# Attention on one core: normalisation steps a period later, one weight step a period, all row sums from a pre-added tile

## The chip, the core and the metric

The kernel runs on one core of a Trainium2 chip. The time is in device microseconds of that core. A profiled execution gives one trace; times in the trace count from the start of its span.

## What is computed

The program chains three stages in float32: an attention with a soft cap, a dense feed-forward layer and a layer with eight experts, of which each token uses one. The change touches the attention alone.

```python
# q, k, v: (4, 12, 448, 64), cap = 30
scores = scale * np.matmul(q, k.transpose(0, 1, 3, 2))
scores = cap * np.tanh(scores / cap)
scores = scores - np.max(scores, axis=-1, keepdims=True)
attn = np.exp(scores)
attn = attn / (np.sum(attn, axis=-1, keepdims=True) + 1e-09)
return np.matmul(attn, v).astype(np.float32)
...
h = x @ w_in                          # x: 1792 tokens x 768
g = np.maximum(h, 0.0) ** 2
x = g @ w_out
```

The kernel leaves out the maximum: with the cap, exp(30) is the most that can come, and the small term 1e-9 is scaled by exp(-cap) to fit (`eps`).

## The kernel before

**Pairs and periods.** The 48 heads are worked on as 24 pairs, `pr` = 0 to 23; two heads of 64 rows fill 128 partitions. A loop with `pr` = 0 to 24 makes the scores of pair `pr` and, one turn late, the values of pair `pr - 1`. A turn of this loop is called a period here. Its instructions are recorded engine by engine in the order of the code, and each engine and each queue works in that order; semaphores make an engine wait for what it needs.

**One period on each engine.** The keys of a head are cut in four chunks: three of 128 keys (one pair of heads gives two score tiles each, `scores`, L198) and a last one of 64, where both heads share one tile (`scores_last`, L213). q and k come as float32 and are split into a high and a low part (`prep`, L61 and L63, on VectorE), so each score is three matmuls. ScalarE takes tanh of the scores from PSUM (L204, L218), and one exp over all seven tiles of a pair (`exps`, L224). TensorE multiplies by the values (`values_last`, L241; `values`, L248) and, with a stationary tile of ones, makes the row sums of exp (L257) in the other half of the same PSUM tile. ScalarE copies one head's result out (`copy_out`, L266, tile `ot`), VectorE the other's (L269, into `x`). Only two PSUM tiles `o` exist, so the next pair's L241 waits for both copies.

**The fold.** VectorE adds chunks of exp together before TensorE sums them (`fold`, L232, tile `w`): where two chunks are added, one add is done and TensorE has two pairs of `ones` matmuls (`o<-t,ones` for the third chunk, `o<-w,ones`); where three are added, two adds and one pair. Before the change three are added in the odd periods below 16, two in the others.

**Normalisation in units of four heads.** `norm_sum` gathers each head's sums through SP in a small tile `den` (L287) and moves the odd head's result to its place in `x` (L289). Then `norm_recip` adds `eps` and takes the reciprocal (L349, L350, VectorE), `norm_spill` writes it to DRAM (`dd`, L354, SP), `norm_spread` reads it back broadcast over 64 partitions (`r`, L362, SP, two DMAs), and `norm_x` multiplies `x` by it (L369, VectorE, two instructions for a unit). The table `when` gives, in half periods, how long after its heads each step is recorded. A step for an even number stands after `values` and ahead of `prep` in the code of its period; one for an odd number stands at the period's end.

**Other work in the attention.** The table `side` puts steps of the feed-forward layer's first weights into periods: three chunks, each with two loads and six steps on VectorE (`w_steps`: L400 to L410 and the split), and six splits of `x` for the first group of tokens (`split_x`). SP also issues the loads of the next pairs: `qkraw` (L177) and `v` (L183).

```python
last = NHD // NU - 2
for u in range(last + 1):
    i0 = NU * (u + 1) + 2
    when = (1, 1, 2, 5, 6)
```

Of the kernel before, what the change touches and what calls it, by code (L numbers as in the profile page):

```python
# [10 lines left out]
F32 = mybir.dt.float32  # L11
# [4 lines left out]
ALU = mybir.AluOpType  # L16
# [4 lines left out]
B, H, S, D = 4, 12, 448, 64  # L21
NHD = B * H
# [7 lines left out]
KC = 4  # L30
KP = 128
KL = S - (KC - 1) * KP
NP, NPC = NHD // 2, 2 * (KC - 1) + 1
QK = S + KC * KP
FOLD_ALL = 32
FB = 2
NU = 4
WARM = 8
# [10 lines left out]
class Kernel:  # L49
# [13 lines left out]
        eng.tensor_tensor(out=lo, in0=src, in1=f32(hi), op=ALU.subtract)  # L63


    def constants(self):
        nc, tc = self.nc, self.tc
        p = self.const
        cap = p.tile([128, 1], F32, name="cap")
        nc.sync.dma_start(out=cap, in_=self.a["cap"].rearrange("(o n) -> o n", o=1).to_broadcast([128, 1]))  # L70
        self.cap = cap

    def scales(self):
        nc, p, cap = self.nc, self.const, self.cap
        self.tscale = p.tile([128, 1], F32, name="tscale")
        nc.vector.reciprocal(out=self.tscale, in_=cap)
        nc.vector.tensor_scalar_mul(out=self.tscale, in0=self.tscale, scalar1=float(D) ** -0.5)
        self.eps = p.tile([128, 1], F32, name="eps")
        nc.scalar.activation(out=self.eps, in_=cap, func=ACTF.Exp, scale=-1.0)
        nc.vector.tensor_scalar_mul(out=self.eps, in0=self.eps, scalar1=1e-9)  # L80

    def gate_loads(self):
        nc = self.nc
# [59 lines left out]
    def attention(self, tail_p):  # L143

        nc, tc, a = self.nc, self.tc, self.a
        with ExitStack() as ctx:
            pool = lambda name, bufs, **k: ctx.enter_context(tc.tile_pool(name=name, bufs=bufs, **k))
            raw_p = pool("araw", 2)
            hl_p = pool("ahl", 2)
            t_p = pool("at", 2)  # L150
            w_p = pool("aw", 2)
# [20 lines left out]
            def load(pr, cuts=(0, QK)):  # L172
                if pr < NP:
                    b, j = divmod(pr, H // 2)
                    raws[pr] = raw_p.tile([128, QK], F32, tag="qk", name="qkraw")
                    for c0, c1 in zip(cuts, cuts[1:]):
                        nc.sync.dma_start(out=raws[pr][:, c0:c1], in_=a["qk"][b, j, :, c0:c1])  # L177

            def load_v(pr):
# [5 lines left out]
            def prep(pr, cuts=(0, QK)):  # L185

                if pr < NP:
                    t = raws.pop(pr)
                    w = hls[pr] = hl_p.tile([128, 2, QK], F32R, tag="hl", name="hl")
                    for c0, c1 in zip(cuts, cuts[1:]):  # L190
                        self.split("dve", "dve", w[:, 0, c0:c1], w[:, 1, c0:c1], t[:, c0:c1])

            def scores(pr, c):

# [28 lines left out]
                t = P[pr]  # L223
                nc.scalar.activation(out=t, in_=t, func=ACTF.Exp, scale=self.cap[:KP])  # L224

            def fold(pr, chunks):

                if chunks > 1:
                    W[pr] = w_p.tile([KP, 2, S], F32, tag="w", name="w")
                    src = P[pr][:, 0:2]  # L230
                    for c in range(1, chunks):
                        nc.vector.tensor_tensor(out=W[pr], in0=src, in1=P[pr][:, 2 * c:2 * c + 2], op=ALU.add)  # L232
                        src = W[pr]


            def values_last(pr):
# [3 lines left out]
                for h, o in enumerate(sums[pr]):  # L240
                    nc.tensor.matmul(out=o, lhsT=last[rows[h]], rhs=P[pr][rows[h], NPC - 1], start=True, stop=False)  # L241

            def values(pr, chunks):

                v, p, o = vs.pop(pr), P.pop(pr), sums[pr]
                for c in range(KC - 1):
                    for h in range(2):
                        nc.tensor.matmul(  # L248
                            out=o[h][rows[h]], lhsT=v[:, 2 * c + h], rhs=p[:, 2 * c + h],
                            start=False, stop=c == KC - 2,  # L250
                        )
                parts = [p[:, 2 * c:2 * c + 2] for c in range(chunks, KC - 1)]
                if chunks > 1:
                    parts.append(W.pop(pr))
                for n, t in enumerate(parts):
                    for h in range(2):
                        nc.tensor.matmul(  # L257
                            out=o[h][rows[1 - h]], lhsT=one, rhs=t[:, h], start=False, stop=n == len(parts) - 1
                        )

            def copy_out(pr, h):
                i = 2 * pr + h
# [7 lines left out]

            cuts = (0, S + KP, QK)
            load(0, cuts)
            self.constants()
            load_v(0)
            load(1)
            load_v(1)
            prep(0, cuts)
            self.scales()
            load(2)
            den = []  # L280

# [11 lines left out]
            last = NHD // NU - 2  # L293
            for u in range(last + 1):
                i0 = NU * (u + 1) + 2
                when = (1, 1, 2, 5, 6)
                for j, f in zip(when, (
                    lambda u=u: self.norm_recip(den[u]),
                    lambda u=u: dd.update({u: self.norm_spill(den[u])}),
                    lambda u=u: r.update({u: self.norm_spread(n_p if u < last else tail_p, dd[u])}),  # L300
                    lambda u=u: self.norm_x(u, r[u], (0,)),
                    lambda u=u: self.norm_x(u, r[u], (1,)),
                )):
                    if u < last or j < 3:
                        steps.setdefault(i0 + j, []).append(f)

            prep(1)
            for pr in range(NP + 1):  # L310
                i = 2 * pr
                chunks = 3 if pr % 2 == 1 and i < FOLD_ALL else 2
                if pr:
                    fold(pr - 1, chunks)
                for c in range(KC - 1):
                    if pr and c == KC - 2:
                        values_last(pr - 1)
                    if pr < NP:
                        scores(pr, c)
                    if not pr and not c:  # L320
                        scores_last(pr)
                if pr < NP:
                    exps(pr)
                if pr:
                    values(pr - 1, chunks)
                    copy_out(pr - 1, 1)
                scores_last(pr + 1)
                for f in steps.get(i, []) + self.side.get(i, []):
                    f()
                prep(pr + 2)  # L330
                if pr:
                    copy_out(pr - 1, 0)
                    if pr % 2:
                        p, bufs = (tail_p, 1) if pr == NP - 1 else (n_p, 2)
                        den.append(p.tile([128, NU * S // 128], F32, tag="den", name="den", bufs=bufs))
                else:
                    load(3)
                load(pr + 4)
                if pr:
                    norm_sum(i - 2)  # L340
                    norm_sum(i - 1)
                load_v(pr + 2)
                for f in steps.get(i + 1, []) + self.side.get(i + 1, []):
                    f()
# [463 lines left out]
def build(ctx, tc, a, stop=None):  # L808
# [9 lines left out]
    with tc.manual_schedule():  # L818
# [10 lines left out]
        k.dram = pool("adr", 2, space=DRAM)  # L829
        tail_p = tc.alloc_tile_pool(name="tail", bufs=1, side="right")  # L830
        side = k.side = {6: [k.gate_loads]}
        at = iter([i for i in range(NU, NHD) if i % NU in (0, 1)])
        chunks = [k.w_steps(*c) for c in (("i", 0), ("i", 1), ("o", 0))]
        side[2] = [chunks[0][0]]
        for n, (_, *rest) in enumerate(chunks):
            for m, f in enumerate(rest):
                i = next(at)
                side.setdefault(i, []).append(f)
                if m == len(rest) // 2 and n + 1 < len(chunks):
                    side[i].append(chunks[n + 1][0])  # L840
        for j, i in enumerate((34, 35, 38, 39, 42, 43)):
            side.setdefault(i, []).append(lambda j=j: k.split_x(0, "dve", "dve", j))
        conv = k.w_conv(*k.chunk(0))
        side.setdefault(43, []).append(lambda: k.w_load(*k.chunk(0)))
# [41 lines left out]
def _layout(i):  # L886
    c = np.ascontiguousarray
    pair = lambda t: t.transpose(0, 1, 3, 2).reshape(B, H // 2, 2 * D, t.shape[2])
    q, k, v = i["q"], i["k"], i["v"]
    n = (KC - 1) * KP  # L890
    last = pair(k[:, :, n:])
    z = np.zeros_like(last[:, :, :D])
    last = np.concatenate([np.concatenate([last[:, :, :D], z], 3), np.concatenate([z, last[:, :, D:]], 3)], 2)
    qk = np.concatenate([pair(q), pair(k[:, :, :n]), last], 3)
    vl = v[:, :, n:].reshape(B, H // 2, 2, KL, 1, D)
    one = np.ones_like(vl[:, :, 0])
    vl = np.concatenate([np.concatenate([vl[:, :, 0], one], 3), np.concatenate([one, vl[:, :, 1]], 3)], 2)
    v = v[:, :, :n].reshape(B, H // 2, 2, KC - 1, KP, D).transpose(0, 1, 4, 3, 2, 5).reshape(B, H // 2, KP, -1, D)
    w_in = c(c(i["moe_w_in"]).reshape(KD, 128, NFC, 128).transpose(2, 1, 0, 3))
    return {  # L900
        "qk": c(qk),
        "v": c(np.concatenate([v, vl], 3)),
        "cap": c(i["cap"]).reshape(1),
        "w_in": w_in.view(np.int64),
        "w_out": c(i["moe_w_out"]).view(np.int64),
        "mod_id": c(c(i["moe2_modality_id"]).reshape(NT // 128, 128).T),
        "w_gate": c(c(i["moe2_w_gate"]).reshape(KD, 128, E).transpose(1, 0, 2)),
        "mod_bias": c(i["moe2_modality_bias"]),
        "w1": c(i["moe2_w1"].reshape(E, KD, 128, NF2, 128).transpose(0, 3, 2, 1, 4)).reshape(E, NF2, 128, DM),
        "w2": c(  # L910
            i["moe2_w2"].reshape(E, NF2 // 2, 2, 128, 2, HALF).transpose(0, 4, 1, 3, 2, 5)
        ).reshape(E, 2, NF2 // 2, 128, DM),
    }
# [14 lines left out]
```

## Time and profile before

| | us |
|---|---|
| median of 3 runs (lowest, highest) | 910.21 (908.96, 910.98) |
| the profiled execution | 908.5 |
| its span | 906.8 |
| TensorE matmul busy | 889.1 (98%) |
| VectorE busy | 565.1 (62%) |
| ScalarE busy | 371.7 (41%) |

The span is the time from the first to the last instruction; the profiled execution is 1.7 us longer and lies within the runs. The shares are means over stages with different limits: in the attention, roughly the first 192 us, ScalarE and VectorE are far busier than over the whole. Matmul ends are modelled, so the starts of instructions are the better thing to read. In the timelines instructions of one kind that follow each other are one row, with their count behind the x; a float32 matmul of the attention's values or sums counts as two.

### The profile page before, as it was taken

Reading aid. Unit: us, or ns where it says so; the run is one execution under the profiler, and the core shown is the slowest. Engines: PE = TensorE matmul, PEld = TensorE weight load, DVE = VectorE, ACT = ScalarE, POOL = GpSimd, SP = SyncE. Lnnn points to the kernel's source line nnn. Section 1 sums busy time; section 2 is a strip of 40 time slices with the busy share of each in tenths; the row PEclk is TensorE's granted clock in tenths of the full one; section 3 lists DMA queues with packets and bytes.
Section 4 is the critical chain, followed back from the end, with each engine's and each line's share of the span. In section 5 each row is a group of like instructions: output and inputs, shape, how many; then the busy total and the mean of one; then the engine's idle time right before and its main releaser. Section 6 shows DMA issues by size and latency. Waiting matters only on the chain.

```text
span 906.8 us, 12105 instructions
## 1 busy us (share of the span) xinstructions
PE 889.1 (98%) x4674; PEld 734.5 (81%) x4675; DVE 565.1 (62%) x1067; ACT 371.7 (41%) x532; POOL 0.6 (0%) x9
## 2 busy tenths in 40 slices
PE   8999989999999999999999999999999999999997
PEld 4554444558989989889898898988978998999997
DVE  6768577667856767676676676554857516336361
ACT  7998878967542332413223232324421111111111
POOL 0000000000000000000000000000000000000000
PEclk9999999999999999999999999999999999999999
DMA  6554655432321111212121121000115424525451
GB/s 200 138 163 125 175 151 144 120 99 92 105 70 48 58 53 53 62 45 69 35 71 53 53 58 48 18 1 0 53 38 168 153 66 135 166 79 162 136 164 48
DMA packets 39571, 83.29 MB, mean 92 GB/s; under 512 B 8656, under 2 KB 16976, under 8 KB 39504
## 3 DMA queue, kind: packets, MB, share of 16 engines
q1 hardware_dynamic: 35472, 76.92, 28.8%
q10 hardware_dynamic: 4032, 5.51, 1.6%
q8 instruction: 39, 0.64, 0.3%
q14 instruction: 28, 0.23, 0.1%
HBM read 73.97 MB, written 5.59 MB: 88 GB/s over the span
## 4 chain that ended last, share of the span: by engine, by line
PE 90%; DVE 4%; ACT 2%; DMA 2%; issue 1%; SPq 0%; DVEq 0%; ACTq 0%
PE h L426 12%; PE h L428 12%; PE h L427 12%; PE y L426 8%; PE y L428 8%; PE y L427 8%; PE o L248 5%; PE o L426 4%; PE o L428 4%; PE o L427 4%; PE s L198 4%; PE o L257 3%; PE o L241 2%; PE s L213 2%; DMA den<-ot 2%
## 5 line engine op out<-in xcount | busy, mean ns | idle before, releaser
L428 PE MATMUL h<-xh,wil 128*128 128x512 f32 (+1 forms) x576 | 208.9, 363 | 0.0
L426 PE MATMUL h<-xh,wih 128*128 128x512 f32 (+1 forms) x576 | 208.8, 363 | 0.0
L427 PE MATMUL h<-xl,wih 128*128 128x512 f32 (+1 forms) x576 | 208.8, 362 | 0.0
L517 DVE TENSOR_TENSOR x<-y,x 128x512 f32<-128x512 f32 (+1 forms) x168 | 103.9, 622 | 70.0 <-PE y L428 68.9
L426 PE MATMUL y<-gh,woh 128*128 128x512 f32 (+1 forms) x384 | 139.6, 364 | 0.5 <-DVE x L517 0.4
L428 PE MATMUL y<-gh,wol 128*128 128x512 f32 (+1 forms) x384 | 139.2, 362 | 0.0
L427 PE MATMUL y<-gl,woh 128*128 128x512 f32 (+1 forms) x384 | 139.1, 362 | 0.0
L493 ACT ACTIVATE r<-h 128x512 f32<-128x512 f32 (+1 forms) x64 | 34.9, 545 | 243.3 <-PE h L428 236.8
L426 PEld LDWEIGHTS h<-xh,wih 128*128 128x128 f32 x576 | 108.2, 188 | 12.5 <-issue 0.7
L427 PEld LDWEIGHTS h<-xl,wih 128*128 128x128 f32 x576 | 108.1, 188 | 11.6
L428 PEld LDWEIGHTS h<-xh,wil 128*128 128x128 f32 x576 | 108.1, 188 | 11.3
L499 DVE TENSOR_TENSOR gl<-r,gh 128x512 fp32r<-128x512 f32 (+1 forms) x64 | 39.7, 621 | 64.8 <-ACT gh L498 64.8
L426 PEld LDWEIGHTS y<-gh,woh 128*128 128x128 f32 x384 | 72.1, 188 | 9.4 <-DVE x L517 0.9
L427 PEld LDWEIGHTS y<-gl,woh 128*128 128x128 f32 x384 | 72.1, 188 | 7.6
L428 PEld LDWEIGHTS y<-gh,wol 128*128 128x128 f32 x384 | 72.1, 188 | 7.5
L426 PE MATMUL o<-w2h,hh 128*128 128x384 f32 x224 | 74.9, 335 | 0.0
L428 PE MATMUL o<-w2h,hl 128*128 128x384 f32 x224 | 74.9, 334 | 0.0
L427 PE MATMUL o<-w2l,hh 128*128 128x384 f32 x224 | 74.9, 334 | 0.0
L204 ACT ACTIVATE t<-s,tscale 128x896 f32<-128x896 f32 x72 | 69.7, 1008 | 9.1 <-PE s L198 8.1
L224 ACT ACTIVATE t<-t,cap 128x3136 f32<-128x3136 f32 x24 | 69.8, 2910 | 0.8
L198 PE MATMUL s<-hl 64*128 64x448 f32 x432 | 62.8, 413 | 0.0
L727 DVE SCALAR_TENSOR_TENSOR hl<-h,hh 128x512 fp32r<-128x512 f32 (+1 forms) x32 | 19.9, 622 | 68.6 <-ACT hh L726 68.6
(122 smaller groups left out, 1022.6 us busy)
## 6 DMA issues: line engine op xcount, KB each, us to landing
raw<-w SPq DMA_DIRECT2D x64, 384.0 KB, 3.2
raw<-w_in SPq DMA_DIRECT2D x32, 384.0 KB, 3.1
raw<-w_out SPq DMA_DIRECT2D x32, 384.0 KB, 3.1
qkraw<-qk SPq DMA_DIRECT2D x23, 480.0 KB, 4.3
v<-v SPq DMA_DIRECT2D x24, 256.0 KB, 2.9
r<-dd SPq DMA_DIRECT2D x24, 224.0 KB, 3.8
out<-o ACTq DMA_DIRECT2D x28, 192.0 KB, 1.8
x<-ot SPq DMA_DIRECT2D x24, 112.0 KB, 2.2
```

The source lines that it names most:

```text
L198: nc.tensor.matmul(out=s[:, h, :S], lhsT=w[rows[h], kp, S + c * KP:S + (c + 1) * KP], rhs=w[rows[h], qp, :S], start=n == 0, stop=n == 2,)
L204: nc.scalar.activation(out=P[pr][:, 2 * c:2 * c + 2], in_=s[:, :, :S], func=ACTF.Tanh, scale=self.tscale[:KP])
L224: nc.scalar.activation(out=t, in_=t, func=ACTF.Exp, scale=self.cap[:KP])
L248: nc.tensor.matmul(out=o[h][rows[h]], lhsT=v[:, 2 * c + h], rhs=p[:, 2 * c + h], start=False, stop=c == KC - 2,)
L257: nc.tensor.matmul(out=o[h][rows[1 - h]], lhsT=one, rhs=t[:, h], start=False, stop=n == len(parts) - 1)
L426: nc.tensor.matmul(out=out, lhsT=wh, rhs=vh, start=first and j == 0, stop=False)
L427: nc.tensor.matmul(out=out, lhsT=wh, rhs=vl, start=False, stop=False)
L428: nc.tensor.matmul(out=out, lhsT=wl, rhs=vh, start=False, stop=last and j == m - 1)
L493: nc.scalar.activation(out=r, in_=ps, func=ACTF.Relu)
L499: split = lambda: nc.vector.tensor_tensor(out=gl, in0=r, in1=f32(gh), op=ALU.subtract)
L517: nc.vector.tensor_tensor(out=y, in0=ps, in1=y, op=ALU.add)
L727: nc.vector.scalar_tensor_tensor(out=hl, in0=ps, scalar=0.0, in1=f32(hh), op0=ALU.max, op1=ALU.subtract)
```

## The change

The three chunks are added in every period, so the branch on `chunks` falls away. The normalisation's steps come one half period later in the table (1, 1, 2, 5, 6 becomes 2, 2, 3, 8, 8, and 2, 2, 3, 7, 7 for the last units), which moves the reciprocal and the spill from the end of a period into the next one. The weight steps go from two in every second period to one in each, the splits of `x` two to four half periods later. The cap no longer has a DMA of its own: it comes as 16 columns ahead of q and k in the first pair's load, and the scales are made between the two cuts of that pair's split.

```diff
-FOLD_ALL = 32
+CP = 16
...
-                    raws[pr] = raw_p.tile([128, QK], F32, tag="qk", name="qkraw")
+                    raws[pr] = raw_p.tile([128, CP + QK], F32, tag="qk", name="qkraw")
                     for c0, c1 in zip(cuts, cuts[1:]):
+                        c0, c1 = CP + c0 if c0 or pr else 0, CP + c1
                         nc.sync.dma_start(out=raws[pr][:, c0:c1], in_=a["qk"][b, j, :, c0:c1])
...
-                        self.split("dve", "dve", w[:, 0, c0:c1], w[:, 1, c0:c1], t[:, c0:c1])
+                        self.split("dve", "dve", w[:, 0, c0:c1], w[:, 1, c0:c1], t[:, CP + c0:CP + c1])
+                        if not pr and not c0:
+                            self.scales(t[:, 0:1])
...
-            def fold(pr, chunks):
-
-                if chunks > 1:
-                    W[pr] = w_p.tile([KP, 2, S], F32, tag="w", name="w")
-                    src = P[pr][:, 0:2]
-                    for c in range(1, chunks):
-                        nc.vector.tensor_tensor(out=W[pr], in0=src, in1=P[pr][:, 2 * c:2 * c + 2], op=ALU.add)
-                        src = W[pr]
+            def fold(pr):
+
+                w = W[pr] = w_p.tile([KP, 2, S], F32, tag="w", name="w")
+                nc.vector.tensor_tensor(out=w, in0=P[pr][:, 0:2], in1=P[pr][:, 2:4], op=ALU.add)
+                nc.vector.tensor_tensor(out=w, in0=w, in1=P[pr][:, 4:6], op=ALU.add)
...
-                parts = [p[:, 2 * c:2 * c + 2] for c in range(chunks, KC - 1)]
-                if chunks > 1:
-                    parts.append(W.pop(pr))
-                for n, t in enumerate(parts):
-                    for h in range(2):
-                        nc.tensor.matmul(
-                            out=o[h][rows[1 - h]], lhsT=one, rhs=t[:, h], start=False, stop=n == len(parts) - 1
-                        )
+                for h in range(2):
+                    nc.tensor.matmul(out=o[h][rows[1 - h]], lhsT=one, rhs=w[:, h], start=False, stop=True)
...
-            self.constants()
...
-                when = (1, 1, 2, 5, 6)
+                when = (2, 2, 3, 8, 8) if i0 + 8 <= NHD else (2, 2, 3, 7, 7)
...
-                    if u < last or j < 3:
+                    if u < last or j < 4:
...
-                chunks = 3 if pr % 2 == 1 and i < FOLD_ALL else 2
...
-        at = iter([i for i in range(NU, NHD) if i % NU in (0, 1)])
+        at = iter(range(NU + 1, NHD, 2))
...
-        for j, i in enumerate((34, 35, 38, 39, 42, 43)):
+        for j, i in enumerate((36, 40, 41, 43, 44, 45)):
```

**The order on SP, two periods (a unit's spill and spread).** The rows are the queue of DMAs that SP issues; `dd` is the spill to DRAM, `r` the spread, numbers tell tiles apart. Before:

```order
L289 DMA x_66<-ot_530 64x448
L183 DMA v_548<-v 128x512
L354 DMA dd_553<-den_405 128x14
L362 DMA r_605<-dd_553 64x2x448 x2
L177 DMA qkraw_614<-qk 128x960
L287 DMA den_542<-x_66 32x1x14
L287 DMA den_542<-ot_596 32x1x14
L289 DMA x_66<-ot_596 64x448
L183 DMA v_619<-v 128x512
L177 DMA qkraw_677<-qk 128x960
```

After the change:

```order
L340 DMA dd_598<-den_402 128x14
L172 DMA qkraw_604<-qk 128x960
L273 DMA den_533<-x_66 32x1x14
L273 DMA den_533<-ot_588 32x1x14
L275 DMA x_66<-ot_588 64x448
L178 DMA v_609<-v 128x512
L348 DMA r_611<-dd_598 64x2x448 x2
L172 DMA qkraw_671<-qk 128x960
```

The spread stood right behind the spill it reads; now five DMAs stand between them, and the spill stands ahead of a load instead of behind `v`.

**The order on VectorE, from one copy-out to the next folds.** `w` is the fold, `hl` the split of q and k, `x<-x,r` the multiplication of the normalisation, `t` and `wih`, `wil` the weight steps. Before:

```order
L269 COPY x<-o 128x448
L369 TENSOR_TENSOR x<-x,r 128x448
L349 TENSOR_SCALAR den<-den,eps 128x14
L350 RECIPROCAL den<-den 128x14
L232 TENSOR_TENSOR w<-t 128x896
L369 TENSOR_TENSOR x<-x,r 128x448
L400 TENSOR_SCALAR t<-raw 128x384
L403 TENSOR_SCALAR t<-t 128x384
L61 CAST hl<-qkraw 128x960
L63 TENSOR_TENSOR hl<-qkraw,hl 128x960
```

After the change:

```order
L226 TENSOR_TENSOR w<-t 128x896
L227 TENSOR_TENSOR w<-w,t 128x896
L335 TENSOR_SCALAR den<-den,eps 128x14
L336 RECIPROCAL den<-den 128x14
L61 CAST hl<-qkraw 128x960
L63 TENSOR_TENSOR hl<-qkraw,hl 128x960
L257 COPY x<-o 128x448
L386 TENSOR_SCALAR t<-raw 128x384
L389 TENSOR_SCALAR t<-t 128x384
L226 TENSOR_TENSOR w<-t 128x896
L227 TENSOR_TENSOR w<-w,t 128x896
L355 TENSOR_TENSOR x<-x,r 128x448 x2
```

The multiplication and the reciprocal stood between the copy-out and the fold; now both stand behind a fold of two adds, in different periods, and only a weight step is left between copy-out and fold.

## Rows read from the trace of the kernel before

**Rows 1.** TensorE timeline: start, us, engine, line, operation; idle time before it in brackets.

```profile
17.52 0.87 PE L213 MATMUL s<-hl 128*128 128x448 f32 x3
...
39.27 0.88 PE L213 MATMUL s<-hl 128*128 128x448 f32 x3
...
41.41 0.91 PE L241 MATMUL o<-t,v 64*128 64x448 f32 x4
...
46.03 0.87 PE L213 MATMUL s<-hl 128*128 128x448 f32 x3
...
53.53 0.88 PE L213 MATMUL s<-hl 128*128 128x448 f32 x3
...
178.80 0.88 PE L213 MATMUL s<-hl 128*128 128x448 f32 x3
...
187.14 1.02 PE L241 MATMUL o<-t,v 64*128 64x448 f32 x4 [0.76 <-ACT ot L266]
```

**Rows 2.** List of waits, 77 to 156.4: total us, times, longest.

```profile
DVE x L369 <- DMA r<-dd: 16.6, 5, 5.1
...
DVE den L349 <- DMA den<-ot: 4.2, 5, 1.2
...
PE o L257 <- DVE w L232: 3.5, 2, 2.5
```

**Rows 3.** Timeline of SP, the queue that issues the DMAs.

```profile
64.28 0.52 SPq L289 DMA_DIRECT2D x<-ot  x1
...
66.01 0.52 SPq L287 DMA_DIRECT2D den<-x  x1
...
69.42 0.52 SPq L289 DMA_DIRECT2D x<-ot  x1
...
70.65 0.39 SPq L354 DMA_DIRECT2D dd<-den  x1
73.07 1.30 SPq L362 DMA_DIRECT2D r<-dd  x2
...
75.08 0.55 SPq L287 DMA_DIRECT2D den<-x  x1
...
79.45 0.52 SPq L289 DMA_DIRECT2D x<-ot  x1
...
98.91 0.52 SPq L287 DMA_DIRECT2D den<-x  x1
...
104.16 0.52 SPq L289 DMA_DIRECT2D x<-ot  x1
```

**Rows 4.** Timeline of ScalarE.

```profile
44.02 2.91 ACT L224 ACTIVATE t<-t,cap 128x3136 f32<-128x3136 f32 x1
46.84 0.51 ACT L266 COPY ot<-o 128x448 f32<-128x448 f32 x1
47.25 0.64 ACT L218 ACTIVATE t<-s,tscale 128x448 f32<-128x448 f32 x1
47.78 2.96 ACT L204 ACTIVATE t<-s,tscale 128x896 f32<-128x896 f32 x3
50.77 2.91 ACT L224 ACTIVATE t<-t,cap 128x3136 f32<-128x3136 f32 x1
53.68 0.53 ACT L266 COPY ot<-o 128x448 f32<-128x448 f32 x1
```

**Rows 5.** Groups by line: busy us, mean ns, idle us before.

```profile
L232 DVE TENSOR_TENSOR w<-w,t 128x896 f32<-128x896 f32 x8 | 8.7, 1092 | 0.3
```

**Rows 6.** Windows: stretch, length, VectorE busy us (instructions), granted clock, DMA.

```profile
17.50:178.70 161.20, 113.59 (x181) 1.00 0.51 145
131.40:178.70 47.30, 34.45 (x57) 1.00 0.47 133
```

**Rows 7.** Timeline of ScalarE at the start.

```profile
6.27 1.01 ACT L204 ACTIVATE t<-s,tscale 128x896 f32<-128x896 f32 x1 [0.43 <-PE s L198]
```

**Rows 8.** DMA issues: KB each, median us to landing.

```profile
qkraw<-qk SPq DMA_DIRECT2D x23, 480.0 KB, 4.3
```

More of the change, by code (lines that the diff above doesn't have):

```diff
@@ L63, in split, with scales @@
         eng.tensor_tensor(out=lo, in0=src, in1=f32(hi), op=ALU.subtract)
[L66 to L74, printed above, removed]
+    def scales(self, src):
+        nc, p = self.nc, self.const
+        cap = self.cap = p.tile([128, 1], F32, name="cap")
         self.tscale = p.tile([128, 1], F32, name="tscale")
-        nc.vector.reciprocal(out=self.tscale, in_=cap)
+        nc.vector.reciprocal(out=self.tscale, in_=src)
         nc.vector.tensor_scalar_mul(out=self.tscale, in0=self.tscale, scalar1=float(D) ** -0.5)
+        nc.vector.tensor_copy(out=cap, in_=src)
         self.eps = p.tile([128, 1], F32, name="eps")
         nc.scalar.activation(out=self.eps, in_=cap, func=ACTF.Exp, scale=-1.0)
-        nc.vector.tensor_scalar_mul(out=self.eps, in0=self.eps, scalar1=1e-9)
     def gate_loads(self):
@@ L241, in values_last, with values @@
                     nc.tensor.matmul(out=o, lhsT=last[rows[h]], rhs=P[pr][rows[h], NPC - 1], start=True, stop=False)
-            def values(pr, chunks):
-                v, p, o = vs.pop(pr), P.pop(pr), sums[pr]
+            def values(pr):
+                v, p, w, o = vs.pop(pr), P.pop(pr), W.pop(pr), sums[pr]
                 for c in range(KC - 1):
@@ L277, in attention @@
             prep(0, cuts)
-            self.scales()
             load(2)
@@ L303, in attention @@
                 )):
-                    if u < last or j < 3:
+                    if u < last or j < 4:
                         steps.setdefault(i0 + j, []).append(f)
             prep(1)
+            nc.vector.tensor_scalar_mul(out=self.eps, in0=self.eps, scalar1=1e-9)
             for pr in range(NP + 1):
                 i = 2 * pr
-                chunks = 3 if pr % 2 == 1 and i < FOLD_ALL else 2
                 if pr:
-                    fold(pr - 1, chunks)
+                    fold(pr - 1)
                 for c in range(KC - 1):
@@ L324, in attention @@
                 if pr:
-                    values(pr - 1, chunks)
+                    values(pr - 1)
                     copy_out(pr - 1, 1)
@@ L893, in _layout @@
     last = np.concatenate([np.concatenate([last[:, :, :D], z], 3), np.concatenate([z, last[:, :, D:]], 3)], 2)
-    qk = np.concatenate([pair(q), pair(k[:, :, :n]), last], 3)
+    cap = np.broadcast_to(c(i["cap"]).reshape(1, 1, 1, 1), last.shape[:3] + (CP,))
+    qk = np.concatenate([cap, pair(q), pair(k[:, :, :n]), last], 3)
     vl = v[:, :, n:].reshape(B, H // 2, 2, KL, 1, D)
@@ L902, in _layout @@
         "v": c(np.concatenate([v, vl], 3)),
-        "cap": c(i["cap"]).reshape(1),
         "w_in": w_in.view(np.int64),
```

## The prediction

> **What bounds the kernel now.** I read the TensorE timeline of the attention first. A period (one pair of heads) runs here from one start of L213 to the next. With two `ones` matmul pairs in it (L257 `o<-t,ones` besides `o<-w,ones`) it takes 53.53 - 46.03 = 7.50 us, with one pair 46.03 - 39.27 = 6.76 [rows 1]; the difference, 0.74, is what the second pair costs. No instruction inside is late: TensorE sets the pace. The stretch from 17.52 to 178.80 [rows 1] holds 21 periods (2 to 22), 14 of the long kind and 7 of the short. At these two lengths they would take 152.32 us; they take 161.28, so 8.96 us are lost to waits.
>
> The list of waits from 77 to 156 says where: VectorE stood 16.6 us for `r<-dd` and 4.2 us for `den<-ot`, and TensorE then 3.5 us for the pre-added `w` [rows 2]. VectorE runs in order, so a multiplication by a late `r` holds up the fold behind it. The queue's timeline says why `r` is late. Two periods on SP went from 64.28 to 79.45, so 15.17 us [rows 3], where TensorE needs 6.76 + 7.50 = 14.26. In them SP stood from 70.65 to 73.07 for its own spill to land before it could issue the spread.
>
> The rest of the program is left alone: after the last attention matmul its order on TensorE is the same, so what is saved before is saved at the end.
>
> **The change, part by part.**
>
> *Fold of three chunks in all periods.* It takes away 16 pairs of `ones` matmuls: one in each long period 2 to 22 (14), one in 23, one in 24. In the 21 periods that is 14 x 0.74 = 10.4 us, if the others keep up with 6.76. In period 23 it is 0.74 more, in 24 another 0.74. At the join of 23 and 24, though, TensorE stood 0.76 us for ScalarE's copy [rows 1]. That copy started 53.68 - 53.53 = 0.15 us after the next L213 where the period was long, and 46.84 - 46.03 = 0.81 where it was short [rows 1, 4]. With short periods throughout it comes 0.66 later, and TensorE waits that much longer. The ends together: 0.74 + 0.74 - 0.66 = 0.82 us.
>
> *ScalarE.* From exp to exp it needed 50.77 - 44.02 = 6.75 us without a wait [rows 4]: equal to TensorE's 6.76 within the reading. It trails by 0.81 and does not fall further back. I cost it at nothing; the cover is thin. That sum goes by starts, which lie before the end of the instruction in front: the tanh at 47.25 starts while the copy (46.84, 0.51) is still running [rows 4]. [...]
>
> *VectorE.* It gains 16 second adds of 1.09 us [rows 5], 14 of them in the 21 periods: 113.59 + 14 x 1.09 = 128.9 us busy [rows 6], 6.14 a period of 6.76. In the last six (17 to 22), where the splits of x are, it is 34.45 + 6 x 1.09 = 41.0, so 6.83 a period [rows 6]: it falls behind by up to 0.4 us in all. Cover: its copy L269 must be done only when TensorE comes to the next L241, 41.41 - 39.27 = 2.1 us later [rows 1]; ScalarE's copy of the same shape takes 0.51 [rows 4]. I take 0; the other end is 0.4. The weight steps are the same 18 with the same instructions, one a period instead of two in every second, which keeps a period's load near the mean. I cost their move at nothing, under the same cover.
>
> *Normalisation moved back.* The reciprocal of four heads runs one period later and now behind the fold, not ahead of it; both multiplications run behind a fold, two to three periods after the spread. The spread is issued a period end after the spill, behind the load, the two den copies, x and v. So no wait for the spill stays: 73.07 - 70.65 - 0.39 = 2.03 us gone from SP. What SP needs for two periods is then, from x to den without the spread 66.01 - 64.28 = 1.73, the spill 0.39 (now ahead of a load), x and v 70.65 - 69.42 = 1.23, spread and load 75.08 - 73.07 = 2.01, and twice from den to x, 69.42 - 66.01 = 3.41 and 79.45 - 75.08 = 4.37 [rows 3]. Sum 13.14, against 2 x 6.76 = 13.52. The new wait is the spill's for the reciprocal, with load, den copies, x and v queued behind it; SP comes to it a den landing and two issues after the den copy, 3.41 + 1.23 = 4.6 us [rows 3] and 0.6 more for the copy before; VectorE reaches the reciprocal after that copy, a weight step and two adds of 1.09 [rows 5], by my estimate about 4 us. I cost the wait at nothing. The three weight loads of two tiles add under 1 us each in periods without a spread. A queue that runs late by less than a period delays nobody, since den and r have a period more than before. So the 8.96 us of stalls go. Late next is ScalarE.
>
> *The cap.* One small DMA goes, the first load is 16 columns wider, and three tiny operations move between the two cuts' splits. The first tanh waited for TensorE's scores, not for the scales [rows 7], so I cost this at nothing. A gain is excluded by that wait; a loss ends at three times the 0.51 of a copy of 448 columns [rows 4], 1.5 us, which is far more than a single column needs.
>
> **Sum.** 161.28 - 21 x 6.76 = 19.3 us, plus 0.82, makes 20.1. The profiled execution would go from 908.5 (span 906.8) to 888.4. The median of the runs stands 1.7 us above that execution, 910.2, so I predict **890**.
>
> **The rivals.**
>
> *ScalarE sets the pace.* If its instructions stop overlapping, the period is 0.51 + 0.64 + 2.96 + 2.91 = 7.02 [rows 4], so 21 x 0.26 = 5.5 us are given back: 895.6. For it: no two short periods follow each other in the trace. Against: the exp-to-exp time of 6.75. Chance 0.08.
>
> *The SP queue stays the bound.* If both den copies need 4.37 us, as behind a spread, two periods cost 5.36 + 8.74 = 14.1, 7.05 each: 21 x 0.29 = 6.1 back, 896.2. For it: every qk row now begins 64 bytes into a pitch of 3904 bytes, where it was 3840 without a gap, and the den copies land behind a qk load of 480 KB that takes 4.3 us [rows 8]. Against: the lag must first eat the added period. Chance 0.08. [...]
>
> *Slower.* The same loop, with the landing of den behind large loads: from den at 98.91 to x at 104.16 it was 5.25 us [rows 3], behind two weight tiles. If every period of the faster attention looked so, two would cost 5.36 + 10.5 = 15.9, 7.93 each, 24.6 us over the sum: 914.7. It decides from 5.0 us on, where the gain is used up. Against: the trace has it only in the few periods with weight loads. Chance 0.04.
>
> *The stalls stay.* If VectorE waits for the normalisation as now, only the matmuls' 11.2 us are gained: 899. The added period speaks against it. Chance 0.03. That gain and loss cancel: 0.02.
>
> **How the numbers follow.** The forecast has 0.75; its own range is 887.5 (a reading error of 0.1 us a period) to 894 (0.1 the other way, 0.4 for VectorE, 1.5 for the start). To reach 8 in 10 I take in ScalarE's case: 887.5 to 896. A measurement of this kernel can tell about 0.2% from no change. Faster by more: 0.75 + 0.08 + 0.08 + 0.03 = 0.94; within: 0.02; slower: 0.04.
>
> **What would show it.** Right: starts of L213 6.7 to 6.8 us apart from period 2 to 22; no wait of VectorE for `r` or `den`; SP's spread issued without a wait; no L257 `o<-t,ones`; ScalarE nearly without idle time; a wait of 1.4 us at the join of periods 23 and 24. Wrong: periods near 7.0 with ScalarE never idle (the first rival), or with TensorE waiting for `w` and VectorE for `den` (the second and third).

## The result, and the profile after

The changed kernel takes 889.65 us (median of 4 runs, 888.20 to 890.41) against 909.62 for the kernel before in the same comparison (908.96 to 910.98): the ratio is 0.9777 with a 95% interval of 0.9758 to 0.9796. The forecast was 890, between 887.5 and 896. The profiled execution took 890.2 us, its span is 888.5, and the mean granted clock 0.999. A second comparison of the same changed kernel gave 889.62 (888.27 to 891.19, 5 runs, ratio 0.9778, 0.9762 to 0.9793).

In the changed kernel the start of a period is line L210 (before L213), the values L235 and L242, the `ones` L247, exp L221, ScalarE's copy L254, VectorE's copy L257, the two adds L226 and L227, the reciprocal L335 and L336, the multiplication L355, the spill L340, the spread L348, the qk load L172, the v load L178, the den copies L273 and x L275.

**TensorE**, timeline of the changed kernel (start, us, engine, line, operation; idle time before it in brackets):

```profile
17.64 0.87 PE L210 MATMUL s<-hl 128*128 128x448 f32 x3
...
24.39 0.87 PE L210 MATMUL s<-hl 128*128 128x448 f32 x3
...
139.08 0.87 PE L210 MATMUL s<-hl 128*128 128x448 f32 x3
...
141.40 0.99 PE L235 MATMUL o<-t,v 64*128 64x448 f32 x3
...
146.11 0.87 PE L210 MATMUL s<-hl 128*128 128x448 f32 x3
...
155.31 0.99 PE L235 MATMUL o<-t,v 64*128 64x448 f32 x3
...
160.01 0.87 PE L210 MATMUL s<-hl 128*128 128x448 f32 x3
...
167.71 1.44 PE L235 MATMUL o<-t,v 64*128 64x448 f32 x4 [0.89 <-ACT t L221]
...
172.24 0.50 PE L412 MATMUL h<-xh,wih 128*128 128x512 f32 x1
```

The first two rows are 6.75 us apart, and from 17.64 to 139.08 there are 18 periods of 6.74 to 6.75. Then come three of 7.03, 7.00 and 6.90. The stretch of 21 periods takes 160.01 - 17.64 = 142.37 us where it took 161.28 [rows 1]: 18.91 less, for a forecast of 19.3. From the last start to the first matmul behind the attention, 172.24 - 160.01 = 12.23, where it was 192.00 - 178.80 = 13.20 (the row at 192.00 is the first matmul `h<-xh,wih` in the timeline of before): 0.97 less, for a forecast of 0.82. The wait at the join is 0.89 and the value matmuls behind it take 1.44, where they took 0.76 and 1.02 [rows 1]: 0.55 more, where 0.66 was forecast.

**How full the engines are**, windows of the changed kernel (stretch, length, then busy us and instructions of PE, PEld, DVE, ACT, POOL; granted clock, DMA share, GB/s):

```profile
60.00:135.00 75.00, 75.00 (x463) 39.44 (x459) 67.74 (x106) 74.18 (x68) 0.00 (x0) 1.00 0.59 165
```

In 75 us of the undisturbed stretch TensorE is busy for all of them, ScalarE for 74.18 and VectorE for 67.74. Two engines are full, and the third has 10% left.

**Waits** from 17 to 162 (engine and line, what it waited for: total us, times, longest):

```profile
DVE x L257 <- PE o L247: 12.3, 16, 1.3
...
DVE den L335 <- DMA den<-ot: 1.4, 2, 0.7
```

VectorE's waits for `r` [rows 2] have no row in this stretch any more, the one for den has shrunk to 1.4 us (the forecast had none), and TensorE no longer waits for `w`. The first row, VectorE waiting for TensorE's sums, is an engine that is ahead: 15 of its 16 waits lie in periods of 6.74 and 6.75.

**ScalarE** in the changed kernel:

```profile
62.87 2.92 ACT L221 ACTIVATE t<-t,cap 128x3136 f32<-128x3136 f32 x1
65.69 0.51 ACT L254 COPY ot<-o 128x448 f32<-128x448 f32 x1
66.09 0.64 ACT L215 ACTIVATE t<-s,tscale 128x448 f32<-128x448 f32 x1
...
69.61 2.91 ACT L221 ACTIVATE t<-t,cap 128x3136 f32<-128x3136 f32 x1
```

From exp to exp it is 69.61 - 62.87 = 6.74 us, the forecast 6.75 [rows 4]. The tanh at 66.09 still starts before the end of the copy (65.69 + 0.51 = 66.20).

**SP**, the queue, an early and a late stretch of the changed kernel:

```profile
37.01 0.33 SPq L172 DMA_DIRECT2D qkraw<-qk  x1
38.64 0.51 SPq L273 DMA_DIRECT2D den<-x  x1
...
40.52 0.50 SPq L275 DMA_DIRECT2D x<-ot  x1
...
125.81 0.52 SPq L273 DMA_DIRECT2D den<-x  x1
...
129.82 0.52 SPq L275 DMA_DIRECT2D x<-ot  x1
...
131.06 1.30 SPq L348 DMA_DIRECT2D r<-dd  x2
132.41 0.58 SPq L172 DMA_DIRECT2D qkraw<-qk  x1
133.09 0.55 SPq L273 DMA_DIRECT2D den<-x  x1
...
137.54 0.52 SPq L275 DMA_DIRECT2D x<-ot  x1
138.17 0.52 SPq L178 DMA_DIRECT2D v<-v  x1
...
140.02 0.53 SPq L273 DMA_DIRECT2D den<-x  x1
...
144.16 0.52 SPq L275 DMA_DIRECT2D x<-ot  x1
...
152.28 0.53 SPq L178 DMA_DIRECT2D v<-v  x1
```

**VectorE**, copies and reciprocals of the same stretches:

```profile
37.99 0.62 DVE L257 COPY x<-o 128x448 f32<-128x448 f32 x1 [1.01 <-PE o L247]
...
118.95 0.63 DVE L257 COPY x<-o 128x448 f32<-128x448 f32 x1 [0.79 <-PE o L247]
...
130.07 0.23 DVE L335 TENSOR_SCALAR den<-den,eps 128x14 f32<-128x14 f32 x1 [0.75 <-DMA den<-ot]
...
133.26 0.62 DVE L257 COPY x<-o 128x448 f32<-128x448 f32 x1
...
144.48 0.23 DVE L335 TENSOR_SCALAR den<-den,eps 128x14 f32<-128x14 f32 x1 [0.66 <-DMA den<-ot]
```

I call *lag* the time from the start of VectorE's copy L257 to the issue of the den copy that reads what it wrote. Early it is 38.64 - 37.99 = 0.65 us: SP waits for VectorE. Late it is 125.81 - 118.95 = 6.86 and 140.02 - 133.26 = 6.76: SP comes a whole period late, and VectorE, at the reciprocal, waits 0.75 and 0.66 us for den. The spread at 131.06 waits for nothing, as forecast. (The spill still stands right behind `v` in the queue, at 138.79; what is new is that the qk load follows it, and not the spread.) But from x to the second next x takes 144.16 - 129.82 = 14.34 us, not the 13.14 of the forecast and more than TensorE's two periods of 13.50.

The last three periods are 7.03 + 7.00 + 6.90 - 3 x 6.75 = 0.68 us too long, and the rows say by what. In the 18 periods ahead of them L235 starts 2.13 us after L210, as before the change (41.41 - 39.27 = 2.14 [rows 1]). At 141.40 it starts 2.32 us after, and at 155.31, where the period begins at 153.11, 2.20. The loads of v that it reads there were issued at 138.17 and 152.28 and took 3.1 and 2.9 us to land, so until 141.3 and 155.2: the queue is so late that TensorE waits for v. In the period between, v is in time, and L235 (at 148.40) comes right behind VectorE's copy, which ends at 147.68 + 0.62 = 148.30; ahead of that copy VectorE had waited 0.66 us for den and split a piece of x. The list of waits puts these three down to ScalarE's tanh (L215), which had ended before. The first wait for den, 0.75 us at 130.07, cost TensorE nothing: the periods around it are 6.75 and 6.74.

The span fell by 18.3 us, but the first matmul behind the attention starts 192.00 - 172.24 = 19.76 us earlier (18.91 + 0.97, less 0.12 for the later start of the stretch). The last activations of the two kernels, before and after, show that the work behind the attention takes as long as it did, within 0.3 us:

```profile
901.24 0.58 ACT L749 ACTIVATE o<-o,gs 128x384 f32<-128x384 f32 x1 [3.58 <-PE o L428]
```

```profile
881.77 0.58 ACT L735 ACTIVATE o<-o,gs 128x384 f32<-128x384 f32 x1 [3.58 <-PE o L414]
```

They lie 19.47 apart. The rest is behind the last activation: 906.8 - 901.24 = 5.6 before, 888.5 - 881.77 = 6.7 in this execution, and 5.5 in the second execution of the changed kernel (span 886.5). So 1.2 us of the difference is scatter between executions; what it consists of the trace does not say.

### The profile page after: what moved, and what is told of

It is laid out like the page before. It is cut to its first block, busy times and chain, and to the rows that moved or that the text cites. A ratio compares the mean times of both kernels' runs of the same rounds, so it can differ in the third digit from the quotient of the medians.

```text
span 888.5 us, 11997 instructions
## 1 busy us (share of the span) xinstructions
PE 876.2 (99%) x4610; PEld 730.4 (82%) x4611; DVE 581.8 (65%) x1084; ACT 367.1 (41%) x532; POOL 0.6 (0%) x9
## 4 chain that ended last, share of the span: by engine, by line
PE 91%; DVE 4%; DMA 2%; ACT 1%; issue 1%; SPq 0%; DVEq 0%
PE h L412 12%; PE h L414 12%; PE h L413 12%; PE y L412 8%; PE y L414 8%; PE y L413 8%; PE o L242 6%; PE s L195 5%; PE o L412 4%; PE o L413 4%; PE o L414 4%; PE s L210 2%; PE o L235 2%; PE o L247 2%; DMA r<-dd 1%; DVE x L503 1%
## 5 line engine op out<-in xcount | busy, mean ns | idle before, releaser
L221 ACT ACTIVATE t<-t,cap 128x3136 f32<-128x3136 f32 x24 | 69.9, 2914 | 0.8
```

## Experiments

The theory I put to the test: TensorE's matmuls and the normalisation's waits are the whole gain; the SP queue is still slower than TensorE, runs later with every period, and is hidden by the period that den and `r` have gained. The rivals: that the gain comes out of one part alone; that the waits that are left are VectorE's own load; that ScalarE has room or the queue no longer matters. All ratios are against the kernel before, run on the same chip in the same comparison (median 909.9 to 910.05). Differences to the changed kernel's 889.65 are taken across comparisons, in which the kernel before differs by 0.3 us.

### Each part undone alone

**The old rule of the fold** (two chunks, three in every second pair up to period 15):

```diff
-                nc.vector.tensor_tensor(out=w, in0=w, in1=P[pr][:, 4:6], op=ALU.add)
+                if pr % 2 == 0 and pr < 15:
+                    nc.vector.tensor_tensor(out=w, in0=w, in1=P[pr][:, 4:6], op=ALU.add)
...
+                parts = [w] if pr % 2 == 0 and pr < 15 else [p[:, 4:6], w]
```

> The changed kernel with the old rule for the fold (three chunks in odd periods below 16, two elsewhere). Theory (the matmuls removed and the stalls removed add up): the periods are 6.75 and 7.50 us again and no stall comes back, so the attention is longer by 14 x 0.74 + 0.8 = 11.2 us: 901. Rival (the longer fold is what lets the rest keep up, all 20 us hang on it): 909.

Measured: 900.11 (899.50 to 900.78), ratio 0.9896 (0.9868 to 0.9923). That is 10.5 us over the changed kernel, for 11.2 by the forecast's terms (10.4 in the periods, 0.82 at the ends). Its periods, TensorE's timeline:

```profile
59.92 0.87 PE L210 MATMUL s<-hl 128*128 128x448 f32 x3
...
67.42 0.88 PE L210 MATMUL s<-hl 128*128 128x448 f32 x3
...
74.17 0.87 PE L210 MATMUL s<-hl 128*128 128x448 f32 x3
```

They are 7.50 and 6.75 long, as before the change, but with no longer ones between them: the waits are gone without the fold's help. At this slower pace (14.25 for two periods) the lag stays at 2.9 to 4.2 us from the seventh pair on, until the qk loads end.

**The old places of the normalisation:**

```diff
-                when = (2, 2, 3, 8, 8) if i0 + 8 <= NHD else (2, 2, 3, 7, 7)
+                when = (1, 1, 2, 5, 6)
...
-                    if u < last or j < 4:
+                    if u < last or j < 3:
```

> The changed kernel with the normalisation's steps at their old places (1, 1, 2, 5, 6). Theory (SP's queue needs 15.17 us for two periods where the spread follows its spill): the queue sets the pace early, starts of L210 come to 7.6 us on average and the time to 905, at least the 9.0 us of the old stalls (898.6) and at most 21 x 0.83 (907); SP waits for dd again. Rival (VectorE's mean load decides, not the waits): near 890.

Measured: 903.97 (901.87 to 906.86), ratio 0.9938 (0.9920 to 0.9956), 14.3 us over the changed kernel. Six periods of 6.75, then up to 10.89. Waits from 17 to 175:

```profile
DVE x L355 <- DMA r<-dd: 8.4, 7, 2.8
PE o L247 <- DVE w L227: 7.6, 5, 3.1
```

The waits of before are back [rows 2], and SP stands 18.7 us for the spill in its list of waits. They cost more than the 8.96 us that they cost before: TensorE now asks for two periods in 13.5 us, where this queue takes 14.5 to 16.0 (x to the second next x, from the sixth pair on), and some of it is TensorE's clock (0.50 from 111.78 to 117.00, behind a wait of 3.1 us), told in the last section. So the parts do not add up: undone alone they cost 10.5 and 14.3, together the change is worth 20.

**The old weight steps** (two in every second period, the splits of x at 34, 35, 38, 39, 42, 43):

```diff
-        at = iter(range(NU + 1, NHD, 2))
+        at = iter([i for i in range(NU, NHD) if i % NU in (0, 1)])
...
-        for j, i in enumerate((36, 40, 41, 43, 44, 45)):
+        for j, i in enumerate((34, 35, 38, 39, 42, 43)):
```

> The changed kernel with the weight steps two in every second period again, and the splits of x at their old places. Theory (VectorE has cover of 1.5 us in a period and its mean load stays): 889.5 to 892, a few periods up to 1 us longer where two steps meet the multiplications. Rival (the even spread is needed for the short period): 894 or more, TensorE waiting for w in most of the eight periods with two steps.

Measured: 893.57 (890.91 to 895.26), ratio 0.983 (0.980 to 0.986). The median is 3.9 us over the changed kernel. The trace (an execution of 890.9) shows 2.2: three periods of 7.05, 7.58 and 7.79, a lag of up to 7.6, and 3.2 us in which VectorE waited for den. The forecast put this move at nothing, and the median lies between the expectation's theory (at most 892) and its rival (894 or more). The reason is neither's. In the first two of the three periods L235 waits for v: it starts at 101.47 and 115.79, and the loads issued at 98.37 and 111.91 took 3.0 and 3.7 us to land. In the third it comes right behind VectorE's copy, which ends at 143.72. TensorE never waits for `w`. The 1.7 us between trace and median stay unexplained.

**The cap as a load of its own:**

```diff
+        nc.sync.dma_start(out=cap, in_=self.a["cap"].rearrange("(o n) -> o n", o=1).to_broadcast([128, 1]))
...
-                    raws[pr] = raw_p.tile([128, CP + QK], F32, tag="qk", name="qkraw")
+                    raws[pr] = raw_p.tile([128, QK], F32, tag="qk", name="qkraw")
```

> The changed kernel with the cap loaded by its own DMA again and without the extra columns. Theory (the start is bound by the scores): within 0.2% of the changed kernel's 889.65, the first L210 of period 1 about 0.1 us earlier. Rival (the pitch of 3904 bytes or the DMA matters): 1 us or more to either side, with the qk load's 4.4 us to landing changed by 0.3.

Measured: 891.12 (888.31 to 892.44), ratio 0.9802 (0.9773 to 0.983). This can't be told from the changed kernel, which lies inside its interval; all 21 periods are 6.75. It is also the kernel without the 64 bytes ahead of the qk rows: there the load lands in a median of 4.3 us, as before the change [rows 8], and in the changed kernel in 4.4:

```profile
qkraw<-qk SPq DMA_DIRECT2D x23, 480.0 KB, 4.4
...
den<-x SPq DMA_DIRECT2D x24, 1.8 KB, 3.9
```

### The new places of the normalisation, one at a time

**The spread directly behind the spill** (the wait for the spill put back, the rest as changed):

```diff
-                when = (2, 2, 3, 8, 8) if i0 + 8 <= NHD else (2, 2, 3, 7, 7)
+                when = (2, 2, 2, 8, 8) if i0 + 8 <= NHD else (2, 2, 2, 7, 7)
```

> The changed kernel with the spread one half period earlier, right behind its spill again (2, 2, 2, 8, 8): the added period stays, the gap goes. Theory (SP's queue is still over its pace in the changed kernel, about 14.1 us for two periods, and the added period only hides its lag, of up to 7 us): with 2 us of standing for the spill the queue needs 16.1, the lag is used up halfway and the second half runs near 8 us a period: 900 to 904. Rival (the added period is all that matters): 890.

Measured: 906.94 (904.47 to 909.24), ratio 0.9971 (0.9955 to 0.9986): 17.3 us over the changed kernel, more than expected. SP stood 20.6 us for the spill; its lag went to 11.45 us. Waits from 17 to 175:

```profile
DVE den L335 <- DMA den<-ot: 19.7, 7, 5.4
...
PE o L235 <- DMA v<-v: 6.9, 3, 4.2
```

The second row is what the expectation lacked: at such a lag it is not only the normalisation that is late but the next loads of v in the same queue, and TensorE waits for them directly.

**The reciprocal half a period earlier:**

```diff
-                when = (2, 2, 3, 8, 8) if i0 + 8 <= NHD else (2, 2, 3, 7, 7)
+                when = (1, 1, 3, 8, 8) if i0 + 8 <= NHD else (1, 1, 3, 7, 7)
```

> The changed kernel with the reciprocal and the spill a half period earlier, at the period's end and ahead of the fold (1, 1, 3, 8, 8). Theory: den has some 4 us less before VectorE waits for it, the queue's lag passes that near period 9, and from there the queue paces at 7.05 us: 892 to 895, VectorE waiting for den. Rival (the queue has room): 890 with no wait for den.

Measured: 895.17 (893.39 to 898.72), ratio 0.9845 (0.9812 to 0.9879): 5.5 us over the changed kernel. The same queue with less room: VectorE waits at lags of about 5 us instead of 7, for the den copies 11.8 us in all in its list of waits from 17 to 175 (at most 4.4 at once), and the reciprocal, which stands ahead of the fold again, holds it up: in the longest period (10.35) TensorE waits 3.4 us for `w`.

**The multiplications earlier** (the spread stays, the room behind it is cut from five half periods to two and three):

```diff
-                when = (2, 2, 3, 8, 8) if i0 + 8 <= NHD else (2, 2, 3, 7, 7)
+                when = (2, 2, 3, 5, 6)
```

> The changed kernel with the multiplications at their old distance (2, 2, 3, 5, 6), which is now close behind the spread. Theory: r lands about 10 us after the period's start plus the queue's lag, VectorE comes for it at 7.4, so it waits 2.7 us or more in every second period against a cover of 1.5: 900 to 905, the wait for r the longest of VectorE's. Rival (r arrives in time): 890.

Measured: 918.86 (915.82 to 919.41), ratio 1.0094 (1.0069 to 1.0119). It is slower than before the change, and the expectation missed it by some 14 us. Waits from 17 to 175:

```profile
DVE x L355 <- DMA r<-dd: 30.5, 8, 6.7
...
PE o L247 <- DVE w L227: 19.5, 7, 5.6
```

VectorE stands up to 6.7 us at a multiplication whose spread SP has only just issued (one at 59.17, the multiplication behind it at 65.77), and the fold behind it holds TensorE. What came on top of the waits is TensorE's clock, told in the last section. Undone one at a time, the room behind the spread is therefore the most valuable part of the move: without it 29 us are lost, without the gap between spill and spread 17, without the room ahead of the reciprocal 5.5. These don't add up.

### Is the queue near its limit?

**The spread issued twice** (a second copy into a tile that nobody reads):

```diff
+        if again:
+            r2 = p.tile([128, NU // 2, S], F32, tag="rx", name="rx")
+            for odd in range(2):
+                src = dd.rearrange("(o j t) n -> o t j n", o=1, t=2)[:, odd]
+                self.nc.sync.dma_start(out=r2[odd * D:(odd + 1) * D], in_=src.to_broadcast([D, NU // 2, S]))
```

> The changed kernel, every spread issued twice (the second into a tile that nobody reads). Theory (queue at 14.1 us for two periods, lag hidden): 15.5 us for two periods, the lag used up near period 12, then 7.75 us a period for ten: 899 to 902. By the forecast's sum for the queue (13.14, so 14.5 with the second spread) the lag would be used up only near the end: 890 to 893. Rival (the queue is no bound): 890.

Measured: 909.36 (median of ten, of which nine lie from 905.10 to 910.95 and one took 3548.6), ratio 0.998 (0.9959 to 1.0001, without that one): the whole gain is used up. Two periods of SP went to 15.6 to 17.8 us, the lag to 11. The first long period (11.50) comes only behind ten of 6.75, when the lag is 10, so the place was as expected; the size was not (899 to 902). As with the spread behind the spill, loads of v and qk come late too (VectorE waits 7.7 us in all for qk); waits from 17 to 175:

```profile
PE o L235 <- DMA v<-v: 10.6, 4, 3.2
```

### The last 0.7 us: the queue or VectorE?

**Splits of x earlier** (VectorE's load is spread from the last six periods to further ahead):

```diff
-        for j, i in enumerate((36, 40, 41, 43, 44, 45)):
+        for j, i in enumerate((28, 36, 40, 44, 45, 46)):
```

> The changed kernel with the splits of x spread out (28, 36, 40, 44, 45, 46), so that no period has two beside a full load. If the longer periods 20 to 22 come from VectorE's load: all periods 6.75, 0.7 us less than the changed kernel. If they come from the queue's lag (theory): they stay, and the lag with them.

Measured: 888.87 (888.16 to 891.63), ratio 0.9774 (0.9757 to 0.9792), against 889.62 for the changed kernel in the same comparison: no difference. The lag still reaches 7.5, VectorE still waits 1.0 us for den, and the last three periods are 6.87, 6.73 and 6.87. So the two that waited for v stay long, and the middle one, which hung on VectorE's copy, is whole; as it is in the second execution of the changed kernel too, VectorE's load can have had a part in that one period at most, and it has none in the lag.

**The load of v between the two den copies** (nothing left out; one line moves):

```diff
                     norm_sum(i - 2)
-                    norm_sum(i - 1)
                 load_v(pr + 2)
+                if pr:
+                    norm_sum(i - 1)
```

> The changed kernel with the load of v issued between the two den copies, inside SP's wait for their landing. Theory: 14.1 us for two periods become about 12.9, under the 13.5 that TensorE needs; the lag stays under 3 us, VectorE never waits for den, all periods 6.75: 0.7 us less than the changed kernel, too little to be told by the times alone. Rival (VectorE's load makes the long periods): the lag falls and periods 20 to 22 stay long.

Measured: 888.68 (888.30 to 890.98), ratio 0.9769 (0.9753 to 0.9785). In time it can't be told from the changed kernel (0.9 us less in the median, intervals that overlap nearly wholly), but its trace can. All periods are 6.73 to 6.75 to the end (the stretch only began later, at 20.06, in this execution of 890.58). SP, and under it VectorE's copies:

```profile
122.00 0.52 SPq L273 DMA_DIRECT2D den<-x  x1
122.61 0.53 SPq L178 DMA_DIRECT2D v<-v  x1
123.19 0.51 SPq L273 DMA_DIRECT2D den<-ot  x1
...
128.95 0.55 SPq L273 DMA_DIRECT2D den<-x  x1
```

```profile
121.34 0.62 DVE L257 COPY x<-o 128x448 f32<-128x448 f32 x1 [1.00 <-PE o L247]
...
128.31 0.62 DVE L257 COPY x<-o 128x448 f32<-128x448 f32 x1
```

The den copies are issued 122.00 - 121.34 = 0.66 and 128.95 - 128.31 = 0.64 us behind VectorE's copy, late in the attention as early: the lag does not grow at all. From den to x it takes 2.61 us on the average of 24, where the changed kernel takes 3.65, and in that time v is issued, where the changed kernel only waited. VectorE waits for den nowhere. With the lag gone the loss at the end is gone; with VectorE's load moved the lag stayed, and 0.2 us of the loss. The edit also issues v itself earlier in the queue, so it can't tell a late v from a late den; the rows of the changed kernel above do. In its second execution, too, the one long period (7.03) is a wait for v, issued at 151.76 and landed 2.8 us later, with L235 at 154.71. The loss itself is small and varies (0.68 and 0.28 in the two executions of the changed kernel, none with the cap as a load of its own, at a lag of 7.0), so the lag is the firmer evidence.

### Has ScalarE room?

**ScalarE's copy done twice:**

```diff
+                    nc.scalar.copy(out=O[i], in_=sums[pr][h])
```

> The changed kernel with ScalarE's copy of the result done twice in each period (one more instruction that starts 0.41 us after the first). Theory (ScalarE has no room at 6.75): periods of 7.16, 21 x 0.41 less the 0.8 us by which it may fall further behind: 7 to 9 us more, 897 to 899. Rival (ScalarE has room in the short period): within 1 us of the changed kernel.

Measured: 899.79 (898.58 to 901.33), ratio 0.989 (0.9872 to 0.9908), 10.2 us over the changed kernel. ScalarE's timeline:

```profile
59.24 2.91 ACT L221 ACTIVATE t<-t,cap 128x3136 f32<-128x3136 f32 x1
...
66.40 2.91 ACT L221 ACTIVATE t<-t,cap 128x3136 f32<-128x3136 f32 x1
```

From exp to exp it is 66.40 - 59.24 = 7.16 us, and so are TensorE's periods (7.14 to 7.17): what ScalarE gets more, all of it shows. It has no room in the changed kernel.

## Why the prediction was right, and which term was off

**The matmuls of the fold.** Right: 10.4 us forecast for the 21 periods. With the fold undone they take 152.31 us (17.16 to 169.47), in the second execution of the changed kernel 141.96 (17.47 to 159.43): 10.35.

**The stalls.** Right: 8.96 us were to go, and they went. Of the forecast's signs, no wait of VectorE for `r` held in the 21 periods (behind them it waits 1.09 us, at 174.15); no wait for den did not quite (0.75 and 0.66). New waits took 0.68 us in the profiled execution and 0.28 in the second one, most of it for loads of v, of which the forecast says nothing.

**ScalarE.** Right, at 6.74 against 6.75, and the doubled copy shows that the thin cover was as thin as said. The overlap of its instructions stayed (the tanh at 66.09 against the copy's end at 66.20), and the 18 periods are 6.74 to 6.75, not the 7.02 of the first rival.

**VectorE.** Of the 0.4 us that the splits were to cost at worst 0.25 came at most (the period of 7.00, in one of the two executions); with the splits moved earlier the time was the same. Its 67.74 us in 75 are 6.09 a period, for a forecast of 6.14.

**The ends and the cap.** The ends gave 0.97 for 0.82. The start lies 0.12 us later (17.64 for 17.52), but starts from 17.16 to 20.06 were seen in kernels with the same code up to there, so that nothing of the cap can be seen in it.

**SP: the term that was mis-sized.** Two periods were summed to 13.14 us; once the queue is late they measured 13.9 to 14.6, on the average 14.2, where no weights are loaded. By the late stretch above: from x to den behind a spread 133.09 - 129.82 = 3.27, forecast 3.24; from den to x 4.45, forecast 4.37; from x to den without a spread 2.48, forecast 2.12; from den to x 4.14, forecast 3.41. So of the 1.20 us that are more, 0.73 are that last landing: the short one of [rows 3] was not to be had at the new pace. Another 0.36 lie between x and den. This is the premise of the second rival, both den copies at about 4.37 and 14.1 in two periods, and yet 889.65 was measured and not its 896.2. The premise held and the conclusion did not, since the argument put against it did: the lag must first eat the added period. The lag began to grow behind the sixth pair (0.66), reached 2.9 two pairs later, behind a load of weights, grew from there by some 0.7 in two periods on the average, which is 14.2 - 13.5, by 1.5 in one period behind the next weight load, and came to 7.8. VectorE, coming to the reciprocal, found den only just landed at a lag of 6.14, and waited for it at 6.86 and 6.76. TensorE waited for v behind lags of 133.09 - 125.91 = 7.18 and 147.43 - 139.62 = 7.81. "A queue that runs late by less than a period delays nobody" is borne out in that, though not for the reason given: den and `r` have a period more than before, while the loads of v in the same queue have gained none, and they were the first to cost TensorE time. The attention ends when it has just got there; the qk loads stop four pairs ahead of the end, and the lag falls. So the forecast had a reserve that it did not know to be nearly used up; that the 24 pairs ended in time was luck.

Why the short landing vanished the rows show in part. On time, den went to x in 1.88 us (38.64 to 40.52 above), with its qk load issued 1.63 us ahead of it; late, the qk load is 0.68 ahead (132.41 to 133.09), and a den copy of 1.8 KB then takes 4.4 us to land (its median is 3.9, near the 4.4 of the 480 KB ahead of it). Both times den landed 0.2 us behind the load: on time the load landed at 37.01 + 3.3 = 40.3 and den at 38.64 + 1.9 = 40.5, late at 132.41 + 4.9 = 137.3 and 133.09 + 4.4 = 137.5. What ties the two landings no row shows; that this den copy lands only behind its load is my reading of these two pairs. By it the late queue made its own next landing later, since it no longer spent the load's flight waiting for VectorE; with v issued between the den copies it was never late (0.64 to 0.66 us), and from den to x it stayed at 2.61 on the average.

**The rows that begin 64 bytes in.** The load measured 4.4 with the 64 bytes and 4.3 without: 0.1 between the medians, which the queue's growth does not need, and the kernel without them was not faster. The change of 0.3 in the rival to the cap's expectation was my estimate, and no run shows it.

**Not settled:** the 1.7 us between trace and median with the old weight steps; the 1.2 us at the end of the program; the share of the steps, which lies between 2.2 and 3.9.

## What to carry to other kernels

A queue in order that is a little slower than the engine it feeds (here 14.2 us for two periods against 13.5) did not show as a wait of TensorE in the first 18 periods. It showed as a lag that grew from 0.65 to 7.8 us, and a stage moved back bought a number of periods, not a pace: read issue minus ready time at the first and the last period before trusting a long loop to it. What paid for the lag first was what had the least room in that queue, here v, and not the steps that were given more. Taking the wait out of the queue, by issuing there what comes next anyway, removed the lag itself (0.64 to 0.66 us to the end), where more slack only hid it. And where two engines are full to 99%, as TensorE and ScalarE are now (75.00 and 74.18 us of 75), the next gain must come from both.

## What the runs showed that I had not expected

A long wait of TensorE cost more than its length. In the kernel with the multiplications earlier, the windows around its longest wait:

```profile
64.42:70.03 5.61, 0.01 (x1) 0.00 (x0) 4.16 (x7) 1.59 (x1) 0.00 (x0) 0.78 0.31 83
70.03:71.72 1.69, 1.69 (x4) 0.30 (x5) 1.62 (x5) 0.00 (x0) 0.00 (x0) 0.50 0.00 0
71.72:73.14 1.42, 1.42 (x5) 0.83 (x4) 1.42 (x3) 0.53 (x1) 0.00 (x0) 0.50 0.07 5
73.14:75.05 1.91, 1.91 (x13) 1.73 (x14) 1.84 (x5) 1.04 (x2) 0.00 (x0) 0.66 0.71 203
```

TensorE did nothing from 64.42 to 70.03; within that stretch the granted clock fell (mean 0.78), and it was 0.50 for the next 3.1 us, 0.66 in the 1.9 after, then full again. The same instructions took 1.69 + 1.42 + 1.91 = 5.02 us there and 0.86 + 0.80 + 1.32 = 2.98 in the next period (78.81 to 81.79): 2.0 us on top of a wait of 5.61. The wait of 0.9 us at the join of the changed kernel left the clock at 1.00. From 17.5 to 178 us the mean granted clock is 1.00 before and after the change, 0.98 with the normalisation's old places and with the spread behind the spill, 0.96 with the spread twice, 0.94 with the multiplications earlier (over the whole span of the same executions 0.998 and 0.999, 0.994 and 0.995, 0.990, 0.987): that is part of why the last three came out slower than I had summed.
